# The last two rows of a weight matrix, loaded and multiplied one by one instead of as a pair

## The chip, the cores and the metric

The kernel runs on one core of a Trainium2 chip. The metric is device time in microseconds (us). "The profile" is a record of one execution: what each engine did and when, the DMA packets, and the semaphore events. Times inside a profile count from the start of its span, which is about 1.2 us shorter than the device time. TensorE is the engine that multiplies matrices, PSUM the memory that its results go to, VectorE the engine that copies the result out in the end. The landing of a piece of the weights is the last of its 16 completion events in the trace, one from each DMA engine. Verdicts of faster or slower are given at 2%.

## The reference, cut to what matters

The reference computes one decode step for one token: a grouped-query attention over a cache of 65,536 positions (32 heads, 4 key/value heads, 128 wide), and beside it an MLP; the sum of both goes out as 1,024 numbers.

```
def _B_ref(x, w1, w2, w3, w4):              # D = 1024, F = 3584
    ...
    h2 = _gelu(_layernorm(x1, axis=-1) @ w3) @ w4      # w4: 3584 x 1024
    return x1 + h2
...
return x + _A_ref(xn, A_k_cache, A_v_cache, A_wq, A_wo) + _B_ref(xn, B_w1, B_w2, B_w3, B_w4)
```

The caches are 128 MiB of the 170 MB that the kernel reads. `w4`, 7 MiB, is the last thing that it reads, and the product with `w4` is the last sum before the output.

## The kernel before: the parts that matter

The kernel is written for each engine's queue by hand, with a small helper that works out waits. Each buffer remembers who wrote it last (`w`) and who read it (`r`). Before an operation on queue `q`, `_deps` waits for the writers of what it reads, and for the writers and readers of what it writes. It makes no exception for a writer on the same queue.

```
def _deps(q, reads, writes):
    for b in reads:
        for s, v in b.w.items():
            q.wait((s, v))
    for b in writes:
        for s, v in b.w.items():      # a writer on q itself is waited for too
            q.wait((s, v))
        for s, v in b.r.items():
            q.wait((s, v))

def _grp(q, fns, reads=(), writes=(), partial=False):
    _deps(q, reads, writes)           # waits before the first
    ...                               # one finish signal after the last of the group
```

The 3,584 rows of `w4` are spread over 128 partitions, 28 "rows" of 1,024 numbers each per partition. One row of all partitions is 256 KB and needs four matmuls, each 256 columns wide, which work side by side in four column strips of TensorE. All add into the same PSUM tile, `OUT_ps`.

```
def out_rows(items, reads, last=False):
    fns = []
    for lhs, rhs in items:                          # one item per row
        for jj in range(4):
            fns.append(... e.matmul(OUT_ps[32 * jj:32 * jj + 1, 0:256], lhs, rhs[:, 256 * jj:256 * jj + 256],
                                    start=False, stop=last, tile_position=(0, 32 * jj), ...))
    _grp(q_pe, fns, reads=reads, writes=[b_OUT], partial=True)

# first row, number of rows, slot of Kn, offset in it
w4_parts = [(0, 14, 0, 0), (14, 8, 1, 0), (22, 4, 1, 8), (26, 2, 0, 14)]

def w4_dma(i):                                      # one transfer per piece, all issued early
    r0, nr, s, o = w4_parts[i]
    load_rows(Kn[:, s, o * D:(o + nr) * D], [b_W4[i]], "w4%d" % i, B_w4, r0, nr)

def w4_pe(i):                                       # one group of 4 * nr matmuls per piece
    r0, nr, s, o = w4_parts[i]
    out_rows([(gh_bf[:, r0 + r:r0 + r + 1], Kn[:, s, (o + r) * D:(o + r + 1) * D]) for r in range(nr)],
             [b_W4[i], b_gh], last=(i == len(w4_parts) - 1))
...
for i in range(len(w4_parts)):
    w4_pe(i)
# then VectorE copies OUT_ps to orow, and one DMA stores it
```

So a piece is three things at once: a transfer, a group of matmuls, and the waits that `_deps` puts before the group.

Of the kernel before, what the change touches and what calls it, by code (L numbers as in the profile page):

```python
# [123 lines left out]
def bass_parallel_sum__gqa_block_cached__mixer_s_mlp__decode_kernel(  # L124
# [30 lines left out]
    with ExitStack() as es:  # L155
# [406 lines left out]
                 (16, lambda: wo_dma(0), 19, lambda: wo_pe(0)), (20, lambda: wo_dma(1), 23, lambda: wo_pe(1))]  # L562
        at_dma = {n: f for n, f, _, _ in w_seq}
        at_pe = {n: f for _, _, n, f in w_seq}
        w4_parts = [(0, 14, 0, 0), (14, 8, 1, 0), (22, 4, 1, 8), (26, 2, 0, 14)]

        def w4_dma(i):
            r0, nr, s, o = w4_parts[i]
# [86 lines left out]
```

## Time and profile before

| | before |
|---|---|
| device time, median of 3 runs | 402.97 us (402.88 to 403.31) |
| span of the profile | 401.6 us |
| DMA, mean over the span | 424 GB/s, 170 MB |
| landing of the 4-row piece of `w4` | 397.54 us |
| landing of the last piece (2 rows) | 398.76 us |
| finish of the last matmul | 399.42 us |

The landings and the finish are semaphore events of the trace. The first lines are from the page of the kernel before: busy time of the first engines, the DMA engines' mean busy share in 40 slices of the span (in tenths), and the shares by engine of the chain of work that ended last.

```profile
span 401.6 us, 5142 instructions
...
PE 187.7 (47%) x2043; PEld 84.2 (21%) x2059; DVE 227.8 (57%) x400; ACT 48.4 (12%) x127; POOL 62.0 (15%) x90
...
DMA  8999999999999999999999999999999999999995
...
DMA 54%; DVE 24%; PE 17%; issue 2%; ACT 2%; another core or an unknown queue 1%; SPq 0%; POOL 0%; ACTq 0%
```

The DMA engines are nearly full until about 394 us, and no compute engine is busy for more than 57%. The kernel lasts about as long as its bytes do, plus a tail after the last byte. At the very end the engines do not finish together: the DMA share is 0.61 from 395.2 to 397.58 us and 0.20 from there to 398.80. Here is the end of the kernel before in the timeline, matmuls alone. The columns are start, duration, engine, line, operation, tiles, count, and in brackets the idle time before it and what ended it.

```profile
390.31 2.30 PE L391 MATMUL OUT_ps<-Kn,gh_bf 128*1 128x256 bf16 x56 [0.18 <-DMA Kn<-in_B_w_dram]
395.21 1.88 PE L391 MATMUL OUT_ps<-Kn,gh_bf 128*1 128x256 bf16 x32 [2.59 <-DMA Kn<-in_B_w_dram]
397.58 1.02 PE L391 MATMUL OUT_ps<-Kn,gh_bf 128*1 128x256 bf16 x16 [0.50 <-DMA Kn<-in_B_w_dram]
398.80 0.60 PE L391 MATMUL OUT_ps<-Kn,gh_bf 128*1 128x256 bf16 x8 [0.20 <-DMA Kn<-in_B_w_dram]
```

Each of the four groups of `w4` begins at the landing of its piece. The end of the chain of waits (start, duration, what) says the same of the last piece: landing, then 0.04 us, then 0.62 us of matmuls. The count there (x7) is of the records on the chain, not of all matmuls.

```profile
374.88 23.88 DMA Kn<-in_B_w_dram
398.76 0.04 issue
398.80 0.62 PE OUT_ps L391 x7
```

### The profile page before, as it was taken

The page shows a single profiled execution, that of the slowest core. Times are in us where ns is not written, and L with a number is a line of the kernel's source. Part 1 is how long each engine was busy: PE and PEld are TensorE (multiplying, and loading weights), DVE is VectorE, ACT ScalarE, POOL GpSimd, SP SyncE. Part 2 cuts the span into 40 slices and gives each one's busy share as a digit, 9 for nine tenths or more (in the row PEclk, how much of TensorE's full clock was granted, in tenths as well). Part 3 has the DMA queues.
Part 4 walks back from the last instruction along what each step waited for, and adds up shares of the span by engine and source line. Part 5 has one row for each costly group of instructions (what it writes and reads, how often), then busy time and mean ns, then how long its engine had stood idle before and what let it go on. Part 6 is the DMA issues. An engine that isn't in the chain of part 4 may idle for free.

```text
span 401.6 us, 5142 instructions
## 1 busy us (share of the span) xinstructions
PE 187.7 (47%) x2043; PEld 84.2 (21%) x2059; DVE 227.8 (57%) x400; ACT 48.4 (12%) x127; POOL 62.0 (15%) x90
## 2 busy tenths in 40 slices
PE   0361445064525745275630966353433545344674
PEld 0250111021103511062110731121111311111142
DVE  0217666277806588255753387676836775778410
ACT  0000211011101011011110011111201111112100
POOL 5000013011211011110310102111110102122110
PEclk9999999999855565555565555665565855656556
DMA  8999999999999999999999999999999999999995
GB/s 353 431 416 433 447 421 419 447 436 421 441 441 420 419 441 437 424 434 436 428 426 444 436 421 428 442 434 427 424 450 418 439 441 424 421 428 431 437 420 217
DMA packets 7088, 170.20 MB, mean 424 GB/s; under 512 B 916, under 2 KB 920, under 8 KB 1048
## 3 DMA queue, kind: packets, MB, share of 16 engines
q1 hardware_dynamic: 6920, 169.87, 98.4%
q8 instruction: 16, 0.26, 0.2%
q14 instruction: 8, 0.07, 0.0%
q10 hardware_dynamic: 144, 0.00, 0.0%
HBM read 169.87 MB, written 0.00 MB: 423 GB/s over the span
## 4 chain that ended last, share of the span: by engine, by line
DMA 54%; DVE 24%; PE 17%; issue 2%; ACT 2%; another core or an unknown queue 1%; SPq 0%; POOL 0%; ACTq 0%
DMA Kn<-in_A_k_cache_dram 43%; DVE X L463 12%; DMA Kn<-in_B_w_dram 6%; DMA Vn<-in_A_wq_dram 5%; PE H_ps L366 4%; DVE pT_f L516 3%; PE S_ps L475 3%; PE OT_ps L523 3%; DVE mrow L482 3%; PE M_ps L366 2%; ACT p_sb L505 2%; PE PT_ps L514 1%; PE M_ps L551 1%; PE OUT_ps L391 1%; DVE Yall L380 1%
## 5 line engine op out<-in xcount | busy, mean ns | idle before, releaser
L463 DVE STREAM_TRANSPOSE X<-Kn 128x1024 f32<-128x1024 f32 x128 | 151.7, 1215 | 64.5 <-DMA Kn<-in_A_k_cache_dram 64.5
L523 PE MATMUL OT_ps<-Vn,pT_f 128*32 128x512 bf16 x512 | 59.9, 620 | 54.1 <-DVE pT_f L516 54.1
L475 PE MATMUL S_ps<-X,Yall 128*32 128x512 bf16 x512 | 58.0, 598 | 17.0 <-DVE X L463 17.0
L488 PE MATMUL MB_ps<-Rm,Lmat 128*128 128x16 bf16 x32 | 6.2, 193 | 87.7 <-DVE Rm L483 87.7
L537 POOL TENSOR_TENSOR O_acc<-O_acc,tmpO 128x513 f32<-128x513 f32 x28 | 32.9, 1176 | 89.1 <-ACT tmpO L531 89.1
L535 POOL TENSOR_SCALAR O_acc<-O_acc,ff 128x513 f32<-128x513 f32 x28 | 19.6, 700 | 150.7 <-ACT ff L510 150.7
L505 ACT ACTIVATE p_sb<-S_ps,brun 128x512 bf16<-128x512 f32 x32 | 22.0, 688 | 173.1 <-DVE brun L503 154.6
L482 DVE TENSOR_REDUCE mrow<-S_ps 128x1 f32<-128x512 f32 x32 | 21.6, 674 | 24.6 <-PE S_ps L475 24.6
L531 ACT ACTIVATE tmpO<-OT_ps 128x512 f32<-128x512 f32 x32 | 19.2, 598 | 107.8 <-PE OT_ps L523 107.8
L475 PEld LDWEIGHTS S_ps<-X,Yall 128*32 128x32 bf16 x512 | 16.5, 126 | 54.7 <-DVE X L463 38.6
L516 DVE STREAM_TRANSPOSE pT_f<-PT_ps 128x512 f32<-128x512 f32 x32 | 22.9, 716 | 7.8 <-PE PT_ps L514 4.2
L523 PEld LDWEIGHTS OT_ps<-Vn,pT_f 128*32 128x32 bf16 x512 | 14.6, 128 | 59.4 <-DVE pT_f L516 42.7
L488 PEld LDWEIGHTS MB_ps<-Rm,Lmat 128*128 128x128 bf16 x32 | 3.3, 103 | 112.2 <-DVE Rm L483 112.2
L514 PE MATMUL PT_ps<-p_sb,permR 128*128 128x512 bf16 x16 | 9.5, 594 | 21.2 <-ACT p_sb L505 21.2
L366 PEld LDWEIGHTS H_ps<-xn_bf,W 128*128 128x128 bf16 x224 | 14.4, 172 | 1.7 <-issue 1.7
L366 PE MATMUL H_ps<-xn_bf,W 128*128 128x1 bf16 x224 | 14.5, 202 | 0.0
L514 PEld LDWEIGHTS PT_ps<-p_sb,permR 128*128 128x128 bf16 x32 | 3.4, 106 | 42.4 <-ACT p_sb L505 42.4
L492 DVE TENSOR_REDUCE Bst<-MB_ps 128x1 f32<-128x16 f32 x32 | 5.6, 174 | 8.3 <-PE MB_ps L488 8.3
L330 PE MATMUL M_ps<-ln_s,ones_f 128*128 128x1 f32 x6 | 1.8, 362 | 17.5 <-DVE ln_s L329 17.5
L533 POOL COPY O_acc<-tmpO 128x513 f32<-128x513 f32 x4 | 2.5, 615 | 47.5 <-ACT tmpO L531 47.5
L551 PE MATMUL M_ps<-O_acc,cb_W 128*128 128x128 f32 x32 | 7.4, 403 | 2.0 <-DVE cb_W L544 2.0
L391 PE MATMUL OUT_ps<-Kn,gh_bf 128*1 128x256 bf16 x112 | 5.8, 370 | 3.5 <-DMA Kn<-in_B_w_dram 3.5
(101 smaller groups left out, 114.0 us busy)
## 6 DMA issues: line engine op xcount, KB each, us to landing
Kn<-in_A_k_cache_dram SPq DMA_DIRECT2D x15, 4096.0 KB, 27.4
Vn<-in_A_v_cache_dram SPq DMA_DIRECT2D x15, 4096.0 KB, 22.3
W<-in_B_w_dram SPq DMA_DIRECT2D x2, 3584.0 KB, 25.1
W<-in_A_wo_dram SPq DMA_DIRECT2D x3, 2048.0 KB, 23.2
Kn<-in_A_wq_dram SPq DMA_DIRECT2D x1, 4096.0 KB, 12.3
Vn<-in_A_wq_dram SPq DMA_DIRECT2D x1, 4096.0 KB, 21.4
W<-in_B_w_dram SPq DMA_DIRECT2D x2, 2048.0 KB, 32.2
Kn<-in_A_k_cache_dram SPq DMA_DIRECT2D x2, 2048.0 KB, 24.8
```

The source lines that it names most:

```text
L366: fns.append(lambda e, j=j, cx=cx: e.matmul(ps_tile[:, c0 + cx:c0 + cx + 1], lhs_fn(j - j0, cx), rhs_fn(j), start=(j == 0 and cx == 0), st ...
L463: _op(q_dve, lambda e, ix=ix: e.transpose(out=X32[:, xs, 1024 * ix:1024 * (ix + 1)], in_=Kn32[:, s, 4096 * half + 1024 * ix:4096 * half + ...
L475: fns.append(lambda e, we=we, cm=cm, mv=mv: e.matmul(S_ps[32 * cm:32 * cm + 32, :], Yall[:, h, we, :, :].rearrange("p a g -> p (a g)"), mv ...
L482: _op(q_dve, lambda e: e.reduce_max(mrow[:, m:m + 1], S_ps[:, :], axis=AX.X), reads=[b_S], writes=[b_mrow[m]])
L505: _op(q_act, lambda e: e.activation(p_sb[:, m, :], S_ps[:, :], ACTF.Exp, bias=brun[:, kn:kn + 1], scale=SCALE, accum_out=tmpO[:, m, 512:513]),
L514: _op(q_pe, lambda e: e.matmul(PT_ps[:, :], permR[:, :], p_sb[:, m, :], start=True, stop=True), reads=[b_p[m], b_const], writes=[b_PT])
L516: _op(q_dve, lambda e: e.transpose(out=pT_f[:, :], in_=PT_ps[:, :]), reads=[b_PT], writes=[b_pT])
L523: fns.append(lambda e, q=q, q4=q4: e.matmul(OT_ps[32 * q4:32 * q4 + 32, :], pT_bf[:, q, :, 1], Vn[:, s, 8192 * half + 512 * q:8192 * half ...
L531: _op(q_act, lambda e: e.activation(tmpO[:, m, 0:512], OT_ps[:, :], ACTF.Copy), reads=[b_OT], writes=[b_tmpO[m]], partial=True)
L535: _op(q_pool, lambda e: e.tensor_scalar(out=O_acc[:, :], in0=O_acc[:, :], scalar1=ff[:, m:m + 1], scalar2=0.0, op0=ALU.mult, op1=ALU.add), ...
L537: _op(q_pool, lambda e: e.tensor_tensor(out=O_acc[:, :], in0=O_acc[:, :], in1=tmpO[:, m, :], op=ALU.add), reads=[b_tmpO[m]], writes=[b_Oacc])
L551: fns.append(lambda e, t=t: e.matmul(M0_ps[:, 128:256], cb_W[:, t, :, :].rearrange("p g i -> p (g i)"), O_acc[:, t * P:(t + 1) * P], start ...
```

## The change

The intent: let the matmuls of row 26 run while row 27 is still on its way, so that after the last landing only one row is left to multiply.

```
-        w4_parts = [(0, 14, 0, 0), (14, 8, 1, 0), (22, 4, 1, 8), (26, 2, 0, 14)]
+        w4_parts = [(0, 14, 0, 0), (14, 8, 1, 0), (22, 4, 1, 8), (26, 1, 0, 14), (27, 1, 0, 15)]
```

By the structure above, this line makes two transfers of one, two groups of matmuls of one, and adds a wait.

## The prediction

> What bounds the kernel. The page puts the mean DMA rate at 424 GB/s, with the DMA engines 90% busy or more in nearly every one of 40 slices; the chain that ended last is 54% DMA. 170 MB at that rate fill the 401.6 us span. No compute engine comes near (VectorE 57%, TensorE 47%). So only the bytes, and the tail after the last byte, matter. The change touches the tail alone.
>
> The tail, from the chain of waits and the timeline of the last 12 us. The four pieces of w4 were all issued by 375.3 us, more than 20 us before the last lands. TensorE starts on them at 390.31 (14 rows), 395.21 (8 rows), 397.58 (4 rows) and 398.80 (2 rows), each time after a DMA wait. After the last landing come 8 matmuls, 0.60 us, the VectorE copy of the result, 0.42 us, and the output store, to 401.6: about 2.8 us, all on the critical path.
>
> What the change does. The last piece (512 KB, one 4 KB run per partition) becomes two of 256 KB (2 KB per partition). Bytes and matmuls (112 on w4) are the same. Added: one DMA issue on SyncE, one wait and one completion semaphore. The order of instructions differs only there.
>
> Gain: the timeline shows 4 matmuls (one row) at 0.38 us and 8 at 0.60, so a second row costs 0.22 us. Row 26 should now land about 0.6 us before row 27 (half of the last piece's 1.22 us), and its 0.38 us of work fits in that wait. After the last landing only one row is left: minus 0.22 us, on the critical path.
>
> Costs:
> - One more issue on SyncE, about 0.43 us, some 20 us before it is needed: nothing.
> - Smaller packets. In the packet records a 4 KB packet takes 159 ns and an 8 KB one 309 ns, so about 9 ns is fixed; I estimate 83 ns for 2 KB by the same line. Back to back, an engine spends 155 ns per 4 KB; 16 packets of 2 KB instead of 8 of 4 KB add an estimated 0.03 to 0.06 us, plus one more 9 ns semaphore packet. The Trainium skill ("DMA: Bandwidth & Descriptors", "Why small descriptors are slow (HBM only)") says that each packet carries a small fixed overhead; the 9 ns agree. This trace has no packet of 2 KB, so this is the least certain step.
> - The wait and the extra end of a matmul group: under 0.05 us, before the last landing.
>
> Sum: about -0.15 us of 403, or -0.04%, less than the spread of the three runs of before (402.88 to 403.31). Predicted time 402.8 us, 402.2 to 403.4 in 8 of 10. Faster by over 2%: 0.003; within 2%: 0.99; slower by over 2%: 0.007.
>
> What would show it. The timeline after should end with two groups of 4 matmuls on w4, at about 398.2 and 398.8, each about 0.38 us, with a short DMA wait between. From the last landing to the end of the last matmul: 0.38 instead of 0.60 us. The issue table should show two of 256 KB. Packets of 2 KB should take about 83 ns. Everything before 390 us should be the same to run-to-run noise.
>
> What would make it wrong. The last landing is set by the slowest of 16 engines: the DMA share falls from 1.00 at 391 us to 0.20 in the last microsecond, so engines finish up to a microsecond apart. If 2 KB packets cost clearly more than the line says, the last landing moves later by more than 0.22 us. If the stagger of the engines shifts from run to run by some tenths, the change can't be seen in the time at all.

## More of the kernel before

The granted clock is the share of its full clock that TensorE ran at, as the trace records it.

The 16 completion events of the last piece come from 395.37 to 398.76 us, and the last of them is the landing.

## The result, and the profile after

| | runs | median | range |
|---|---|---|---|
| before, same rounds | 6 | 402.95 us | 402.86 to 403.31 |
| after | 6 | 403.33 us | 403.15 to 403.53 |

The ratio is 1.0008 (95% interval 0.9996 to 1.0021), the same within 2%. A ratio is the mean time of one kernel's runs over that of the other's runs of the same rounds, so it is not quite the ratio of the medians. The measured time lies in the predicted range, but on the other side of before: about 0.34 us were added (difference of the means of these runs), where 0.15 were to be saved.

Lines of the page and of the issue table of the kernel after. The issue table gives tile, engine, operation, count, KB of each and us from issue to landing.

```profile
span 402.1 us, 5144 instructions
...
Kn<-in_B_w_dram SPq DMA_DIRECT2D x1, 1024.0 KB, 23.7
Kn<-in_B_w_dram SPq DMA_DIRECT2D x2, 256.0 KB, 23.9
```

The tail in the timeline of the kernel after, matmuls alone:

```profile
397.80 1.02 PE L391 MATMUL OUT_ps<-Kn,gh_bf 128*1 128x256 bf16 x16 [0.54 <-DMA Kn<-in_B_w_dram]
398.99 0.38 PE L391 MATMUL OUT_ps<-Kn,gh_bf 128*1 128x256 bf16 x4 [0.16 <-PE OUT_ps L391]
399.54 0.38 PE L391 MATMUL OUT_ps<-Kn,gh_bf 128*1 128x256 bf16 x4 [0.17 <-PE OUT_ps L391]
```

Look at what ended the idle time before the two groups of 4. It is no longer a DMA. It is `PE OUT_ps L391`: TensorE waited for itself. The end of the chain of waits of the kernel after has turned over in the same way:

```profile
374.11 23.65 DMA Kn<-in_B_w_dram
397.76 0.04 issue
397.80 1.05 PE OUT_ps L391 x16
398.85 0.14 issue
398.99 0.41 PE OUT_ps L391 x4
399.40 0.14 issue
399.54 0.41 PE OUT_ps L391 x4
```

In the kernel before, the chain passes through the landing of the last piece. Here it leaves DMA one piece earlier, at the landing of the 4-row piece, and stays on TensorE: 16 matmuls, a gap, 4 matmuls, a gap, 4 matmuls. The landings of rows 26 and 27, 398.38 and 398.99 us by the semaphore events, are not on it. Row 26 had to wait 0.6 us for TensorE, and row 27 had landed 0.54 us before its first matmul.

A sum from the landing of the 4-row piece to the finish of the last matmul, with both profiles' own numbers:

| | before | after |
|---|---|---|
| to the last landing | 1.22 | (1.23, off the chain) |
| to the first matmul | 0.04 | 0.04 |
| group of the 4-row piece | (1.05, off the chain) | 1.05 |
| gap, group of row 26 | | 0.14 + 0.41 |
| gap, last group | 0.62 | 0.14 + 0.41 |
| sum (of the unrounded numbers) | 1.89 | 2.19 |

The sum grows by 0.30 us, about what the times show. I call this sum "the tail" below. The two profiles' spans differ by more, 0.53 us, because the 4-row piece landed 0.22 us later in the second profile (397.76 against 397.54 us). The experiments show that this part comes and goes from profile to profile.

### The profile page after: what moved, and what is told of

It is laid out like the page before. It is cut to its first block, busy times and chain, and to the rows that moved or that the text cites. A ratio compares the mean times of both kernels' runs of the same rounds, so it can differ in the third digit from the quotient of the medians. Undisturbed runs are those within 1.5% of the kernel's fastest.

```text
span 402.1 us, 5144 instructions
## 1 busy us (share of the span) xinstructions
PE 188.7 (47%) x2043; PEld 84.5 (21%) x2059; DVE 227.8 (57%) x400; ACT 48.3 (12%) x127; POOL 61.9 (15%) x90
## 4 chain that ended last, share of the span: by engine, by line
DMA 54%; DVE 24%; PE 17%; issue 2%; ACT 2%; another core or an unknown queue 1%; POOL 0%; SPq 0%; ACTq 0%
DMA Kn<-in_A_k_cache_dram 43%; DVE X L463 12%; DMA Kn<-in_B_w_dram 6%; DMA Vn<-in_A_wq_dram 5%; PE H_ps L366 4%; DVE pT_f L516 3%; PE OT_ps L523 3%; PE S_ps L475 3%; DVE mrow L482 3%; PE M_ps L366 2%; ACT p_sb L505 2%; PE OUT_ps L391 1%; PE PT_ps L514 1%; PE M_ps L551 1%; DVE Yall L380 1%
## 5 line engine op out<-in xcount | busy, mean ns | idle before, releaser
L391 PE MATMUL OUT_ps<-Kn,gh_bf 128*1 128x256 bf16 x112 | 6.8, 410 | 3.3 <-DMA Kn<-in_B_w_dram 2.9
```

## The experiments

Theory A: the change loses through the boundary between two groups of matmuls. A group waits until TensorE has finished the one before, so two groups cannot overlap. Theory B: it loses through the smaller transfers. Theory C: the stream of loads came late in the one profile, and nothing else happened. Every run below gave the correct output, and was timed in 5 rounds beside the kernel before (9 runs of it per set of rounds; over all rounds 33 runs of before, 402.72 to 403.31 us).

### One half: two transfers, one group

```
+ # w4_parts as in the change; w4_pe(3) multiplies both rows in one group of 8
+ if i == 3:
+     nr, bufs = 2, [b_W4[3], b_W4[4]]
```

> Half of the change: rows 26 and 27 come in two transfers of 256 KB, but are multiplied as one group of 8 that waits for both. Theory A (the extra time comes from the boundary between two matmul groups: each group on OUT_ps waits until TensorE has finished the group before it): the tail is that of the kernel before, from the last landing to the end of the last matmul about 0.66 us, and the time is that of before plus only what 2 KB packets cost, 0.04 to 0.06 us: a ratio of about 1.0001. Theory B (the extra time comes from the smaller transfers: 2 KB packets, one more completion): the time is that of the change, about +0.35 us, a ratio of about 1.0008. Theory C (the stream of all loads was simply late, by about 0.2 us, in the profile of the change): the first three w4 landings differ between runs by some 0.2 us whatever the kernel, and the tail after them tells A from B.

Measured: 402.92 us against 402.93, ratio 1.0000 (0.9988 to 1.0013). The end of its chain of waits:

```profile
375.28 23.46 DMA Kn<-in_B_w_dram
398.74 0.09 issue
398.83 0.62 PE OUT_ps L391 x7
```

The chain ends on a landing again and on 0.62 us of matmuls, as before. The tail is 1.96 us, 0.07 more than before: 0.02 up to the last landing, and 0.05 from there to the first matmul (0.09 in place of 0.04), where the group now has three waits. Theory B falls. The two transfers cost next to nothing, and this run also clears the extra issue and the extra completion signal of the change.

### The other half: one transfer, two groups

```
+ w4_pe(3, 0, 1)      # row 26, group of 4
+ w4_pe(3, 1, 1)      # row 27, group of 4; both wait for the one transfer of 512 KB
```

> The other half: rows 26 and 27 in one transfer of 512 KB as before, but multiplied as two groups of 4. Theory A: from the last landing to the end of the last matmul 0.04 + 0.41 + 0.13 + 0.41 = about 1.0 us in place of 0.66 (0.41 us from first matmul to the finish signal of a group of 4, 0.13 us from that signal to the next group's first matmul, both read from the profile of the change), so +0.33 us, a ratio of about 1.0008. Theory B: no difference to before, ratio 1.0000.

Measured: 403.27 us against 402.93, ratio 1.0007 (0.9994 to 1.0019). The chain:

```profile
398.94 0.04 issue
398.98 0.41 PE OUT_ps L391 x4
399.40 0.04 issue
399.44 0.41 PE OUT_ps L391 x4
```

Two groups of 4 take 0.41 + 0.04 + 0.41 us, where one group of 8 takes 0.62. The tail is 2.12 us, 0.24 more than before. So a loss of most of that size comes with the group boundary alone. One number was missed: the gap between the groups was 0.04 us and not the expected 0.13. The second group has only one wait left here, since its transfer has been waited for already. A later run takes this up.

### The whole change without the wait

```
-    _grp(q_pe, fns, reads=reads, writes=[b_OUT], partial=True)
+    if drain:
+        _grp(q_pe, fns, reads=reads, writes=[b_OUT], partial=True)
+    else:      # groups of rows 26 and 27: no wait for TensorE's own signal
+        _done(_grp(q_pe, fns, reads=reads), [], [b_OUT], partial=True)
```

Taking this wait away should not be a race: the matmuls of one group add into `OUT_ps` one after another without waits, and the next group's are simply the next in the same queue. The Trainium skill ("PSUM — Partial Sum Buffer", "Engine vs sequencer instructions") says that matmuls start and complete in program order, so that PSUM writes land in issue order. The trace of this run agrees: the finish signals of the last three groups come in that order, at 398.63, 398.85 and 399.13 us. The outputs were correct in all four kernels of this text without the wait, which fits but proves nothing by itself.

> The whole change, but the groups of rows 26 and 27 no longer wait for TensorE's own finish signal of the group before (matmuls that add into the same OUT_ps follow each other on one engine in order; inside a group they have no wait either). Theory A: the last group starts at the landing of row 27 or right behind row 26's matmuls, whichever is later; in the terms of the profile of the change the last matmul ends about 399.3 to 399.5 us instead of 399.95, so about 0.5 us less than the change and about 0.15 us less than before (ratio to before about 0.9996). Theory B: no gain against the change, ratio to before still 1.0008. Correct output either way.

Measured: 402.68 us against 402.93, ratio 0.9995 (0.9981 to 1.0009). The chain:

```profile
397.54 0.04 issue
397.58 1.24 PE OUT_ps L391 x20
398.82 0.00 issue
398.82 0.31 PE OUT_ps L391 x4
```

The gaps are gone. Row 26 follows the 4-row piece without a stop (20 matmuls in one stretch), and row 27 starts 0.04 us after its landing (398.77 us by the semaphore event). The tail is 1.59 us, 0.60 shorter than that of the change and 0.30 shorter than before. Some of this came from the clock: in this profile TensorE was granted its full clock just for the last group (0.31 us), where all others so far had half the clock there (0.41). Therefore the same kernel was run again:

> The change without the two waits, once more, to see whether the gain of 0.25 us over before repeats: about 402.7 us, ratio 0.9995. The profile of the first time granted TensorE its full clock just for the last group (0.31 us); at half clock it should be 0.41 us, and the gain about 0.15 to 0.2 us.

Measured: 402.78 us against 403.13, ratio 0.9992 (0.9979 to 1.0004). The end of its chain is one stretch of all 24 matmuls:

```profile
397.65 1.64 PE OUT_ps L391 x24
```

In this profile the last group took 0.41 us and the tail was 1.68 us, 0.20 shorter than before. So the saving that was predicted for the change is there in the traces as soon as the wait is not. Whether the full clock was chance stays open: it came at 398.77 us in the first of these profiles, at 399.13 in the second and at 398.78 in that of the 3 + 2 + 1 cut without the wait (below), all three before the last matmul was done, and in the tail of none of the ten other profiles.

### The change once more

No edit: the one line of the change, again.

> The change again, unaltered, on the same chip and in the same rounds as the others, as the yardstick: about +0.35 us against before (ratio 1.0008). Theory C (late stream in one profile): the DMA part of the tail, up to the landing of the 4-row piece, should come about 0.2 us earlier in this profile if the first was late by chance, and the time should then come closer to before; theory A says that the time stays near +0.3 us since TensorE, from the landing of the 4-row piece on, is behind: 1.05 + 0.13 + 0.41 + 0.13 + 0.41 us.

Measured: 403.20 us against 402.93, ratio 1.0007 (0.9994 to 1.0019). The 4-row piece landed at 397.59 us, 0.17 earlier than in the first profile of the change, yet the tail was 2.19 us, the same to 0.01. Behind the 4-row piece the chain is the same as well:

```profile
398.68 0.14 issue
398.82 0.41 PE OUT_ps L391 x4
399.23 0.14 issue
399.37 0.41 PE OUT_ps L391 x4
```

Theory C falls as the cause of the added time: it explains 0.2 us of the difference of two spans, and nothing of the tail. Over the ten profiles here, other than that of before, that have the 4-row piece, it landed between 397.50 and 397.83 us, early and late ones with either way of loading the last rows.

### The suspected cost, enlarged

```
+ # the last piece, one transfer as before: 8 groups of 1 matmul, each with a wait for the one before
+ for r in range(nr):
+     for jj in range(4):
+         _op(q_pe, <matmul r, jj>, reads=[b_W4[i], b_gh], writes=[b_OUT], partial=True)
```

> The suspected cost enlarged until it stands clear of the noise: transfers as before (four, the last of 512 KB), but its 8 matmuls form eight groups of one, each with the wait for the group before. Theory A: each group costs the full 0.41 us from its matmul to its finish signal plus the 0.043 us from signal to next matmul that the run with only the matmuls split showed: 8 x 0.41 + 7 x 0.043 = 3.6 us after the last landing in place of 0.62, so about +2.9 us, a ratio of about 1.007. Theory B (transfers) and C (late stream): no change, 1.000.

Measured: 405.84 us against 403.01, ratio 1.0067 (1.0054 to 1.0079). This is the one experiment whose interval stands clear of 1. The chain repeats the same two lines eight times:

```profile
398.98 0.04 issue
399.03 0.39 PE OUT_ps L581
399.41 0.04 issue
399.46 0.39 PE OUT_ps L581
```

A matmul whose end is waited for takes 0.39 us to its finish signal, and 0.04 us later the next starts. 8 x 0.39 + 7 x 0.04 is 3.4 us, against 0.62 when the eight overlap.

### The enlarged groups without the wait

```
- _op(q_pe, <matmul r, jj>, reads=[b_W4[i], b_gh], writes=[b_OUT], partial=True)
+ ev = _op(q_pe, <matmul r, jj>, reads=[b_W4[i], b_gh], writes=[], partial=True)   # signal, but no wait
+ _done(ev, [], [b_OUT], partial=True)
```

> The same eight groups, each with its finish signal, but without the wait for the group before. Theory A: the wait is the whole cost, the signals are nearly free, so the 8 matmuls take 0.62 us as in the kernel before: ratio 1.000 (0 to +0.1 us). A rival D (the count of groups and of their signals costs, not the wait): still about +2.9 us.

Measured: 403.03 us against 403.01, ratio 1.0001 (0.9988 to 1.0014). Its chain ends with:

```profile
398.82 0.04 issue
398.86 0.70 PE OUT_ps L581 x8
```

0.70 us in place of 0.62: within each four matmuls the signals follow each other 0.03 us apart. So it is not the number of groups or of signals that costs, it is the wait for them. The rival D falls.

### The order of two waits

```
+ if swap:                              # groups of rows 26 and 27
+     _deps(q_pe, [], [b_OUT])          # wait for TensorE's own signal written first
  _grp(q_pe, fns, reads=reads, ...)     # then the wait for the transfer
```

> The whole change, with all its waits, but in the groups of rows 26 and 27 the wait for TensorE's own signal is written before the wait for the transfer, not after it. In the profile of the change 0.135 us pass from the finish signal of one group to the first matmul of the next, in the run with only the matmuls split, where there is one wait, 0.043. Theory W1 (the signal that comes last, TensorE's own, is taken by a separate wait instruction, and the transfer's by the weight load; written the other way round, the separate one has passed already): 0.04 to 0.05 us in place of 0.135 at both boundaries, so 0.18 us less than the change, about +0.15 us against before (ratio 1.0004). Theory W2 (two waits cost 0.135 us in whichever order): like the change, +0.3 us.

Measured: 403.19 us against 403.01, ratio 1.0003 (0.9989 to 1.0017). The chain:

```profile
397.83 0.04 issue
397.87 1.05 PE OUT_ps L391 x16
398.92 0.04 issue
398.97 0.41 PE OUT_ps L391 x4
399.38 0.04 issue
399.42 0.41 PE OUT_ps L391 x4
```

Both gaps fell from 0.14 to 0.04 us, as W1 said; the tail is 2.00 us, 0.19 less than the change and still 0.12 more than before. So by these profiles more than half of what the change added, 0.19 of 0.30 us, hangs on the order of the two waits, and the rest on waiting at all. The trace shows why. A group with two waits has an extra semaphore instruction of 0.05 us ahead of its first weight load. In the change its record begins 0.03 us after TensorE's own finish signal (398.88 after 398.85 us), and the weight load follows 0.08 us after that. In this run it begins 0.03 us after the landing of row 27 (399.08 after 399.05 us) and is over long before the finish signal at 399.38. The Trainium skill ("Perfetto Trace Analysis", "Identifying Dependency Chains") says that such instructions may be inserted where one instruction waits on several engines; the trace agrees. What it costs depends on which wait ends last.

### The kernel before without the wait

```
  # w4_parts as in before: 14 + 8 + 4 + 2 rows
- _grp(q_pe, fns, reads=reads, writes=[b_OUT], partial=True)
+ _done(_grp(q_pe, fns, reads=reads), [], [b_OUT], partial=True)     # group of the last piece alone
```

> The kernel before (pair kept) without the wait of its last group for the group before. Theory A: nothing gained, since there the landing of the last piece (398.76 us) comes 0.13 us after the finish signal (398.63 us) and so ends the wait anyway: ratio 1.000, and 0.66 us from landing to finish. If it gains like the split without the wait (0.25 us), then that gain came from the wait alone and not from splitting.

Measured: 403.04 us against 403.01, ratio 1.0001 (0.9989 to 1.0014), and a tail of 1.89 us, that of before. There the wait for the group before has ended 0.13 us before the last landing, so it costs nothing. Splitting alone gains nothing (it loses), taking the wait away alone gains nothing, and both together save 0.2 us or more of the tail.

### Other cuts

With the waits kept, the rows can be cut so that TensorE is hardly behind: 3 + 2 + 1 in place of 4 + 1 + 1.

```
- (22, 4, 1, 8), (26, 1, 0, 14), (27, 1, 0, 15)
+ (22, 3, 1, 8), (25, 2, 0, 14), (27, 1, 1, 11)
```

> All waits kept, the last six rows of w4 cut 3 + 2 + 1 in place of 4 + 1 + 1 (the change) or 4 + 2 (before), five transfers as in the change. Theory A: what made the change a loss is that after the landing of the 4-row piece TensorE needs 1.05 us for it, longer than the next row takes to land (0.62 us), so the two last groups run one after the other behind it. Here the 3-row piece lands about 0.6 us earlier and is done before the 2-row piece lands, that one runs 0.04 + 0.62 us from about 0.61 us before the last landing, so its finish signal comes about 0.05 us after the last landing, then 0.135 + 0.41: about 0.60 us from last landing to finish, in place of 0.66 (before) and 0.96 (the change). Time: about -0.05 us against before (ratio 0.9999), 0.3 us less than the change. A rival E (five groups in place of four cost 0.3 us wherever the cuts are): like the change, ratio 1.0007.

Measured: 402.93 us against 403.13, ratio 0.9996 (0.9983 to 1.0010). The chain:

```profile
398.21 0.04 issue
398.25 0.63 PE OUT_ps L391 x8
398.88 0.14 issue
399.01 0.41 PE OUT_ps L391 x4
```

The last group still waits for TensorE's own signal, but that comes only 0.05 us after the last landing (398.88 after 398.82 us). From that landing to the finish it is 0.60 us, against 0.66 before and 0.96 for the change. The same number of groups, boundaries and transfers as in the change, placed elsewhere, does not lose. Rival E falls by this profile (the interval of the ratio would still allow its 1.0007): what counts is where the boundaries come.

The same cut, with the two last groups not waiting for TensorE's own signal (the edit of the whole change without the wait):

> The 3 + 2 + 1 cut without the waits of the two last groups for TensorE's own signal: last landing + 0.04 + 0.31 to 0.41 us (full or half granted clock), 0.2 to 0.3 us less than before, ratio 0.9993 to 0.9995: the same as the 4 + 1 + 1 cut without these waits, since there too the last landing was what the last group waited for.

Measured: 402.81 us against 403.13, ratio 0.9992 (0.9980 to 1.0005), and 0.35 us from the last landing to the finish, of which the last group took 0.31 us at full granted clock. This is no better than the 4 + 1 + 1 cut without the waits.

All tails in one table. For the runs with the 3 + 2 + 1 cut there is no 4-row piece, so of the tail only the last column applies.

| kernel | ratio of times | tail, us | tail minus before | last landing to finish |
|---|---|---|---|---|
| before | 1 | 1.89 | | 0.66 |
| after, first and second set | 1.0008, 1.0007 | 2.19, 2.19 | +0.30, +0.31 | 0.96, 0.97 |
| two transfers, one group | 1.0000 | 1.96 | +0.07 | 0.72 |
| one transfer, two groups | 1.0007 | 2.12 | +0.24 | 0.91 |
| after, no wait, first and second set | 0.9995, 0.9992 | 1.59, 1.68 | -0.30, -0.20 | 0.35, 0.45 |
| before, no wait | 1.0001 | 1.89 | 0.00 | 0.67 |
| eight groups | 1.0067 | 4.67 | +2.78 | 3.45 |
| eight groups, no wait | 1.0001 | 1.97 | +0.08 | 0.75 |
| after, waits in the other order | 1.0003 | 2.00 | +0.12 | 0.78 |
| 3 + 2 + 1 | 0.9996 | | | 0.60 |
| 3 + 2 + 1, no wait | 0.9992 | | | 0.35 |

A ratio of 1.0007 is 0.28 us of 403. A ratio comes from five or six runs and a tail from one profile, yet "tail minus before" gives the ratio within 0.15 us throughout. Apart from the eight groups with the wait, no interval of a ratio excludes 1, so the times alone would not have settled it.

Three kernels have medians 0.2 us or more below that of before in the same rounds: the split without the two waits (by 0.25 and 0.35 us; ratios 0.9995 and 0.9992), the 3 + 2 + 1 cut without them (0.32; 0.9992) and the 3 + 2 + 1 cut with all waits (0.20; 0.9996). None of these ratios has an interval that excludes 1, so the times alone do not show a gain over before; what the tails show of it is in the table. Ten runs of the first span 402.52 to 402.84 us, and the 18 runs of before in the same rounds 402.72 to 403.27.

## Why the prediction was right or wrong

- **The bound and the place: right.** DMA fills the span, and only the tail moved. The total, 403.33 us, lies in the predicted range. That the time hit the range is no merit of the account of the change: the range is 1.2 us wide, and an unchanged kernel (402.95 us) lies in it too.
- **The direction: wrong.** The point was -0.15 us, and +0.29 and +0.34 were measured (differences of means, in two sets of rounds). Each of these two ratios has an interval that includes 1; that the change loses rests on the tails of its two profiles, +0.30 and +0.31 us.
- **The step that failed** is the third of the costs, "The wait and the extra end of a matmul group: under 0.05 us, before the last landing", together with the claim under the gain that the 0.38 us of row 26 "fits in that wait". Both took row 26 to start at its landing. It could not: TensorE was at work on the 4-row piece until 398.85 us, and row 26 landed at 398.38. The profile of before already had this. Its timeline shows that piece's matmuls until 398.60, and half of 1.22 us after 397.54 is 398.15, so row 26 would land while TensorE was still busy. From there on, the wait for TensorE's own finish signal made each further group pay its full length and a gap, 0.14 + 0.41 = 0.55 us, where one more row inside a group costs 0.22. Of the 0.14 us, 0.09 came from the order in which the two waits are written. The wait stands in `_deps`, and the trace of before shows it: ahead of the last group a semaphore instruction begins at 398.66 us, 0.03 after TensorE's own finish signal (398.63). The prediction counted it as one more wait and did not ask what it would be waiting for.
- **The gain: right in mechanism, not reached by the change.** "After the last landing only one row is left: minus 0.22 us" is what the split without the wait shows (0.45 us from landing to finish in place of 0.66, and 0.35 where the last group ran at the full granted clock).
- **The size of a row: right.** In before, 4 more matmuls add 0.22 us at half the granted clock. The Trainium skill ("TensorE: Matmul & The Clock Gate", "Back-to-back issue gap") gives the gap between matmuls in ns as columns divided by 1.2 for the cold clock, an estimate of 213 ns for 256 columns; the traces agree, with the third and fourth four matmuls of the 4-row piece each 0.21 us after the four before (the second four come 0.17 us after the first).
- **The packets: right, and the cost mis-sized.** A 2 KB packet took 84 ns (83 estimated). The last 512 KB landed 1.23 us after the 4-row piece as two transfers (mean of six profiles, 1.22 to 1.24), against 1.22 as one (five profiles, 1.21 to 1.22): 0.01 us in place of the estimated 0.04 to 0.07.
- **The signs that were named:** two groups of 4 of 0.38 us came as said, but at 398.99 and 399.54 in place of 398.2 and 398.8, and without a DMA wait between them. "From the last landing to the end of the last matmul: 0.38 instead of 0.60" was 0.96 (0.66 in before, on the same count).
- **The risk that was named**, a late landing from slower packets, did not come. The stagger that varies from run to run did: the last landing fell between 398.74 and 399.05 us over the eleven profiles with the 4-row piece. One figure there was too small: "up to a microsecond apart" was read from the falling DMA share, but the completion events of the last piece in before lie 3.4 us apart (395.37 to 398.76).

## What to carry to other kernels

Before cutting the last piece of a stream finer, look at whether the engine that consumes it is idle when the new first part lands; if the piece before is still in work, cut that one too (3 + 2 + 1, not 4 + 1 + 1: 0.60 against 0.96 us after the last landing here). A wait of an engine for its own finish signal, put there by a general dependency helper, was free here while something else ended later, and cost the whole overlap of two groups once it didn't; where the engine runs the two in order anyway it can go. If two waits must stay, their order can matter: here the one that ends last was 0.09 us cheaper when it was written first. When an effect is below the noise, compare intervals inside the traces, and enlarge the suspected cost until the times show it as well.

## What the Trainium skill lacked or had wrong

- "TensorE: Matmul & The Clock Gate": has the time of a matmul alone and of one in a stream, but no line on a group of matmuls that waits for TensorE's own finish signal. Here the gap from signal to next matmul was 0.04 us with one wait and 0.14 us with two, and one row cost 0.55 us in place of 0.22 because groups no longer overlapped.
- "Perfetto Trace Analysis", "Identifying Dependency Chains": says that extra semaphore instructions may be inserted, and gives no cost. Here it was 0.09 us when its wait ended last, and nothing when the waits were written in the other order.
- "TensorE: Matmul & The Clock Gate", "Why this matters for your kernels": puts each further finish signal at about 26 ns; here, at half the granted clock, four signals of matmuls that ran side by side came 34 ns apart (run with eight groups and no wait).
- "DMA: Bandwidth & Descriptors", "Bandwidth": advises batches of at least 1 MiB and has 341 GB/s for 1 MB. That figure is of transfers issued from GpSimd; those of this kernel are issued from SyncE, and cutting the last 512 KB in two delayed the last landing by about 0.01 us. Row 27 of the change, 256 KB queued behind other transfers, landed 0.615 us after row 26. That is the pace of the last of the 16 engines (its 2 KB packets were 80 ns apart, eight to a row), not a rate of all: from 397.60 to 398.60 us they moved 102 GB/s together. The table has no line for a transfer that is queued behind others, where the landing is that of the last engine.
